# Output sums in place, full-height transposes at the end, constant products between the batches, and a new issue order, in a Branchformer block with its gradients

## The chip, the core and the metric

The kernel runs on one core of one Trainium2 chip. The metric is the time of one execution on the device, in microseconds (us); lower is better. The core has five engines with queues of their own: TensorE (PE in the profile, its weight loads PEld), VectorE (DVE), ScalarE (ACT), GpSimd (POOL) and SyncE (SP), which here issues nearly all DMAs. Each engine takes the instructions of its queue in order and waits on semaphores for the others.

## The reference, cut

The program computes a Branchformer block for 2 sequences of 4000 tokens with 144 channels, and the gradients of its input and of all seven weights: nine outputs.

```python
def _fwd_reference(x, w_qkv, w_att_out, w_mlp_in, dw_csgu, w_mlp_out, dw_merge, w_merge):
    xa = _layernorm(x, axis=-1)
    q, k, v = split(einsum('btd,de->bte', xa, w_qkv))
    scores = einsum('btd,bsd->bts', q, k) * D ** (-0.5)
    p = _softmax(scores, axis=-1)
    glob = einsum('btd,de->bte', einsum('bts,bsd->btd', p, v), w_att_out)
    h = _gelu(einsum('btd,de->bte', _layernorm(x), w_mlp_in))
    u, g = h[..., :D], _layernorm(h[..., D:])
    gc = sum over 5 taps of shifted g * dw_csgu[i]
    loc = einsum('btd,de->bte', u * gc, w_mlp_out)
    m = concat([glob, loc])
    m = m + sum over 5 taps of shifted m * dw_merge[i]
    return x + einsum('btc,cd->btd', m, w_merge)

def reference(..., grad_out):
    _out, _vjp = jax.vjp(_f, x, w_qkv, w_att_out, w_mlp_in, dw_csgu, w_mlp_out, dw_merge, w_merge)
    return (_out, *_vjp(grad_out))
```

## The kernel before

Tokens lie on 125 partitions, 32 blocks of 125 tokens to a batch (`NB`), in eight groups of four blocks (`GB`) where inputs are loaded or outputs stored. The two batches run one after the other, each in four stages.

*Preparation* (`pre_pieces`): x and grad_out are loaded; statistics on VectorE (`st`, `mv`), a power on GpSimd, the normalized rows on VectorE, GpSimd and, in the first batch, ScalarE (`ln`, L433 to L437); then transposes of the normalized rows (`xat`, L442 and L446) and of grad_out (`gm`, L400; `gs`, L407) on TensorE, with evictions by ScalarE and VectorE (L447, L408). Ahead of the first batch stands the head: weight products, and 111 constant products (`WARM`, L154) whose result nobody reads.

*Attention with its backward* (`phase_att`): for each of 32 query tiles the scores in four quads of 500 columns (L1026, with the 16 channels above 128 at L1032); the minimum of their negatives on VectorE (L1050, reduced at L1052); the exponentials on ScalarE (L1058, four to a tile); a DMA transpose of P (L1062); the products Y (L1082); P times dP (L1068 to L1073); a DMA transpose of S in two halves (`st0`, `st1`, L1253); the products Z (L1128); and the products X (L1173), which are summed into `acc` on VectorE (L1179). Pieces of the local branch (`local_units`) stand between them.

*Merge* (`class Merge`): the gradient matrix H is summed in PSUM (L1458) while `tr_pieces` transposes the merged rows (L1379, L1384, evicted by ScalarE). `out_g(g)` computes four blocks of the output: it loads x (L1547), forms 48 products (L1555 and L1557) into two PSUM tiles, adds x on VectorE (L1558) and stores (L1559). For the first batch it runs during the second batch's preparation and first query tiles. Loads use two buffers and sums two others, by turns. `dx_a` and `dx_b` form the gradient of x (L1583, L1584, L1586), `dm1` one weight gradient (L1533).

*Final* (`class Final`), after the second batch alone: weight gradients from H. `weights` and `transp` transpose weights of 144 rows in two parts, 128 rows and 16 (L1613, L1614, L1639, L1640, L1645, L1646); `dwm` (L1763 to L1785) runs twice, `qk` between.

All of this is emitted in one natural order, and then `Planner.plan` cuts the instructions into 7,033 groups, checks that `ORDER` names every group once, and chains the groups of each engine in the order that `ORDER` writes out. `ORDER` is a table of group numbers, stored as differences, one list for each of the five queues. A group on TensorE is a run of products into the same tile (up to 16), a quad (up to 8), or one constant product. So the table alone says which instruction each engine takes next; what an instruction waits for comes from the data. PSUM is in three pools: `ps_sg` (two buffers of two banks, for the quads), `ps_w` (three buffers, for nearly everything else) and `ps_yz` (one buffer, for Y and Z and for the constant products).

Two memory regions matter. `SX` holds S for three tiles, then the transposed P from column 12288, the transposed S from 16384 to 20480 and, from 20480, four slots of scaled q rows. In the merge the same columns hold merged rows, the output weights `VU` from 17384, the two x buffers from 19112 to 20264, and the two sum buffers from 20480 to 21632.

Of the kernel before, what the change touches and what calls it, by code (L numbers as in the profile page):

```python
# [8 lines left out]
BF = mybir.dt.bfloat16  # L9
F32 = mybir.dt.float32  # L10
# [5 lines left out]
D = 144  # L16
# [454 lines left out]
WARM = 111  # L471
# [251 lines left out]
for _s in """  # L723
PE 10 1 1 1 1 1 1 1 1 1 1 1 1 1 1 1 1 1 1 1 1 1 172 3 -174 1 1 1 174 2 11 -186 1 1 1 1 1 1 1 1 1 1 1 1 1 1 1 1 1 1 1 1 1 1 1 1 185 2 -186 1 1 1 1 1 1
# [663 lines left out]
class Merge:  # L1388
# [35 lines left out]
    def late_y(self):  # L1424
# [10 lines left out]
        o += 10 * D  # L1435
        self.VUs = [k.SX[0:80, o + D * h:o + D * (h + 1)] for h in range(2)]
        o += 2 * D
        self.xo = [k.SX[0:PB, o + GB * D * h:o + GB * D * (h + 1)].rearrange("p (a b) -> p a b", b=D) for h in range(2)]
        o = 20480
        self.o_ = [k.SX[0:PB, o + GB * D * h:o + GB * D * (h + 1)].rearrange("p (a b) -> p a b", b=D) for h in range(2)]  # L1440

# [347 lines left out]
def kernel(ctx, tc, x, w_qkv, w_att_out, w_mlp_in, dw_csgu, w_mlp_out, dw_merge, w_merge, grad_out,  # L1789
# [159 lines left out]
    for g in range(5, k.NG):  # L1949
        M.dx_a(g)  # L1950
    for g in range(k.NG):
        M.dx_b(g)
    M0 = M
    M.close()
    es_x0.close()

# [81 lines left out]
```

## Time and profile before

| | us |
|---|---|
| median of three runs | 1287.12 (1286.42 to 1287.43) |
| profiled execution | 1286.85 |
| its span, first to last instruction | 1285.1 |
| mean granted TensorE clock | 0.992 |
| idle before TensorE's instructions from 60 to 560 us, ended by another engine or a DMA | 3.6 |

The page gives busy time for each engine, the chain of work that ended last (followed back from the last instruction, at each step to what released it), and groups of instructions by line. A busy TensorE is not TensorE at its peak: its products are pipelined, and a product's own length (0.226 us for 144 columns) is longer than the step from one start to the next (0.062). Costs on TensorE are therefore read from starts. By stage, with times from the start of the span: head 0 to 40, first attention 40 to 575, first merge and second preparation 575 to 630, the first batch's output and the second attention's start 630 to 690, second attention to 1190, second merge and the final part to the end.

### The profile page before, as it was taken

How to read it: one execution, taken by the hardware profiler on the slowest of the kernel's cores; microseconds unless marked ns; L12 is line 12 of the kernel's file. 1: busy time of each engine (PE TensorE's matmuls, PEld its weight loads, DVE VectorE, ACT ScalarE, POOL GpSimd, SP SyncE). 2: the span in 40 equal slices, each digit the busy share in tenths (PEclk: the TensorE clock that was granted, in tenths of full speed). 3: DMA queues.
4: the chain of work that ended last, by engine and by line, in shares of the span. 5: the costliest groups of instructions: out<-in, count | busy, mean ns of one | idle time of the engine just before them, and what ended most of it. 6: DMA issues, size and time to landing. Idle time of an engine off the chain costs nothing.

```text
span 1285.1 us, 38822 instructions
## 1 busy us (share of the span) xinstructions
PE 1252.2 (97%) x15809; PEld 1037.1 (81%) x15809; DVE 1050.0 (82%) x2825; ACT 760.5 (59%) x1232; POOL 479.7 (37%) x971
## 2 busy tenths in 40 slices
PE   9999999999999999999888999999999999999996
PEld 7777888777888888899777788888878888888995
DVE  8698888978888988879668888888979798887755
ACT  5866656666666565536546665666666666555362
POOL 8544334333433342314524334433343343233020
PEclk9999999999999999999899999999999999999998
DMA  4698899998889998984349888999897988989612
GB/s 127 121 159 156 152 153 153 140 161 156 150 157 154 147 159 148 161 195 112 84 96 157 149 162 147 154 155 160 138 163 140 157 155 146 164 144 182 175 57 59
DMA packets 630206, 186.50 MB, mean 145 GB/s; under 512 B 612337, under 2 KB 624972, under 8 KB 630022
## 3 DMA queue, kind: packets, MB, share of 16 engines
q1 hardware_dynamic: 629271, 183.57, 78.8%
q8 instruction: 123, 2.02, 0.6%
q14 instruction: 56, 0.45, 0.1%
q0 software_dynamic: 208, 0.25, 0.1%
q10 hardware_dynamic: 548, 0.21, 0.1%
HBM read 20.82 MB, written 14.22 MB: 27 GB/s over the span
## 4 chain that ended last, share of the span: by engine, by line
PE 82%; DVE 10%; DMA 3%; issue 1%; ACT 1%; POOL 1%; SPq 0%; DVEq 0%; ACTq 0%; POOLq 0%
PE X L1173 20%; PE ps L1026 15%; PE yz L1128 9%; PE yz L1082 9%; PE ps L1032 6%; PE Hps L1458 4%; PE po L1555 3%; DMA SX<-SX 2%; DVE Pb L1050 2%; DVE acc L1179 1%; PE pj L989 1%; PE pc L607 1%; PE pw L667 1%; PE pd L555 1%; PE pd L622 1%
## 5 line engine op out<-in xcount | busy, mean ns | idle before, releaser
L1050 DVE TENSOR_SCALAR_CACHE_REDUCE Pb<-ps 125x1000 bf16<-125x1000 f32 x256 | 306.1, 1196 | 86.1 <-PE ps L1032 84.6
L1058 ACT ACTIVATE Pb<-Pb,nm 125x1000 bf16<-125x1000 bf16 x256 | 278.9, 1127 | 113.5 <-DVE nm L1052 113.2
L1173 PE MATMUL X<-SX 125*125 125x144 bf16 x2048 | 296.5, 229 | 1.6 <-ACT l_sq L523 0.8
L1173 PE MATMUL X<-SX,Pb 125*125 125x144 bf16 x2048 | 291.9, 226 | 0.2 <-POOL SX L1110 0.2
L1071 ACT CAST SX<-ps 125x1000 bf16<-125x1000 f32 x189 | 188.0, 994 | 158.3 <-PE ps L1032 156.3
L1173 PEld LDWEIGHTS <-SX 125*125 125x125 bf16 x2048 | 259.4, 137 | 25.2 <-issue 24.5
L1026 PE MATMUL ps<-xaT_m,qt 128*125 128x500 bf16 x1024 | 261.0, 375 | 2.1 <-DVE Pb L1050 1.7
L1173 PEld LDWEIGHTS <-Pb 125*125 125x125 bf16 x2048 | 260.4, 137 | 2.8 <-issue 2.4
L1179 DVE TENSOR_TENSOR acc<-X,acc 125x432 f32<-125x432 f32 (+1 forms) x372 | 199.1, 549 | 31.6 <-PE X L1173 29.6
L1128 PE MATMUL yz<-xa_aug,SX 125*125 125x144 bf16 x2048 | 152.1, 228 | 5.8 <-DMA SX<-SX 3.3
L1026 PEld LDWEIGHTS <-qt 128*125 128x125 bf16 x1024 | 122.3, 137 | 42.7 <-issue 4.0
L1128 PEld LDWEIGHTS <-SX 125*125 125x125 bf16 x2048 | 139.5, 138 | 13.7 <-issue 7.7
L1082 PE MATMUL yz<-xa_aug,SX 125*125 125x145 bf16 x2048 | 145.3, 227 | 1.0 <-DMA SX<-Pb 1.0
L1082 PEld LDWEIGHTS <-SX 125*125 125x125 bf16 x2048 | 136.5, 137 | 3.3 <-issue 2.0
L1073 DVE TENSOR_TENSOR SX<-SX,Pb 125x1024 bf16<-125x1024 bf16 x189 | 130.8, 695 | 7.7 <-ACT SX L1071 7.1
L1032 PEld LDWEIGHTS <-qt 16*125 16x125 bf16 x1024 | 36.5, 128 | 99.5 <-issue 99.5
L1032 PE MATMUL ps<-XR,qt 16*125 16x500 bf16 x1016 | 111.7, 420 | 0.0
L1068 DVE TENSOR_TENSOR SX<-ps,Pb 125x1000 bf16<-125x1000 f32 x67 | 80.0, 1194 | 9.0 <-ACT SX L1071 5.2
L650 POOL TENSOR_TENSOR A_dwc<-l_fl,A_dwc 128x512 f32<-128x512 f32 (+2 forms) x48 | 37.8, 787 | 85.6 <-ACT l_fl L649 85.6
L632 POOL TENSOR_SCALAR l_w<-gd,nc,c 125x144 f32<-125x144 bf16 x64 | 30.1, 475 | 87.8 <-DVE c L630 80.9
L1001 POOL COPY qz<-qz 125x48 bf16<-125x48 bf16 (+1 forms) x124 | 33.9, 289 | 66.2 <-ACT qz L991 65.4
L1555 PE MATMUL po<-SX 128*125 128x144 bf16 x640 | 54.1, 229 | 2.4 <-DVE SX L1558 2.4
(485 smaller groups left out, 2284.7 us busy)
## 6 DMA issues: line engine op xcount, KB each, us to landing
go_h<-in_grad_out_dram SPq DMA_DIRECT2D x4, 567.0 KB
Yg<-ug_d SPq DMA_DIRECT2D x4, 567.0 KB
Yn_d<-yn SPq DMA_DIRECT2D x64, 35.2 KB
Zn_d<-qz SPq DMA_DIRECT2D x64, 35.2 KB
ug_d<-ugr SPq DMA_DIRECT2D x32, 70.3 KB
SX<-in_x_dram SPq DMA_DIRECT2D x16, 140.6 KB
out_dram<-Pb SPq DMA_DIRECT2D x16, 140.6 KB
out_dram<-SX SPq DMA_DIRECT2D x16, 140.6 KB
```

What stands on the lines that cost most here:

```text
L1026: mm = nc.tensor.matmul(pp[r // 2][:, r % 2, 0:CH], QT[i][:, 3 * h, 0:PB], xaTm[:, c * CH:(c + 1) * CH], start=True, stop=False)
L1032: nc.tensor.matmul(pp[r // 2][:, r % 2, 0:CH], QT[i][rs, 1 + h, 0:PB], xr, start=False, stop=True)
L1050: nc.vector.tensor_scalar(pv(Pbuf, i % NPB, c2), src, -1.0, 3.0e38, op0=ALU.mult, op1=ALU.min, accum_out=NM[i][:, c2:c2 + 1])
L1058: nc.scalar.activation(v, v, ACT.Exp, bias=NM[i][:, 4:5], scale=-1.0)
L1068: nc.vector.tensor_tensor(pv(Sbuf, i % NDB, c2), src, pv(Pbuf, i % NPB, c2), op=ALU.mult)
L1071: nc.scalar.copy(pv(Sbuf, i % NDB, c2), src)
L1073: nc.vector.tensor_tensor(sc, sc, pchunk(i % NPB, c2), op=ALU.mult)
L1082: nc.tensor.matmul(Y, PT[0:PB, j, 0:PB], xaa[:, j, 0:D + 1], start=(j == 0), stop=(j == NB - 1))
L1128: nc.tensor.matmul(Z, ST[0:PB, j, 0:PB], xaa[:, j, 0:D], start=(j == 0), stop=(j == NB - 1))
L1173: nc.tensor.matmul(X[:, jj, :], l, r, start=(n_ == 0), stop=(n_ == len(ops) - 1))
L1179: nc.vector.tensor_tensor(av, X[:, 0:nj, :], av, op=ALU.add)
L1555: nc.tensor.matmul(po[:, q, :], self.yt(h, i + kk), VU[h][:, kk, :], start=(n_ == 0), stop=False)
```

## The change

Four edits, and a new table.

`out_g` adds into the x buffer itself, and takes one of four buffers by turns: the two at 19112 and the two at 20480 that held the sums. A load then overwrites a buffer whose store, four groups earlier, has to be done; in the kernel before it overwrote one that the add of two groups earlier had read.

```diff
-        self.xo = [k.SX[0:PB, o + GB * D * h:o + GB * D * (h + 1)].rearrange("p (a b) -> p a b", b=D) for h in range(2)]
-        o = 20480
-        self.o_ = [k.SX[0:PB, o + GB * D * h:o + GB * D * (h + 1)].rearrange("p (a b) -> p a b", b=D) for h in range(2)]
+        self.xo = [k.SX[0:PB, q + GB * D * h:q + GB * D * (h + 1)].rearrange("p (a b) -> p a b", b=D) for q in (o, 20480) for h in range(2)]
...
-        xo, o_ = self.xo[g % 2], self.o_[g % 2]
+        xo = self.xo[g % 4]
         nc.sync.dma_start(xo, tok_view(k.x, b)[:, b0:b0 + GB, :])
...
-            nc.vector.tensor_tensor(o_[:, 2 * p2:2 * p2 + 2, :], po[:], xo[:, 2 * p2:2 * p2 + 2, :], op=ALU.add)
-        nc.sync.dma_start(tok_view(k.out0, b)[:, b0:b0 + GB, :], o_)
+            nc.vector.tensor_tensor(xo[:, 2 * p2:2 * p2 + 2, :], po[:], xo[:, 2 * p2:2 * p2 + 2, :], op=ALU.add)
+        nc.sync.dma_start(tok_view(k.out0, b)[:, b0:b0 + GB, :], xo)
```

The transposes of `Final` take 128 rows in both parts; the 112 rows under the 16 are zero, and their columns of the result are not copied out.

```diff
-        pt = self.pt([128, 2, D], BF)
+        pt = self.pt([128, 2, 256], BF)
         for cc, (a, w) in enumerate(((0, 128), (128, DR))):
-            nc.tensor.transpose(pt[0:w, cc, 0:128], src[:, 0, c0 + a:c0 + a + w], ident[:])
-            nc.tensor.transpose(pt[0:w, cc, 128:D], src[0:DR, 1, c0 + a:c0 + a + w], ident[0:DR, 0:DR])
-        nc.scalar.copy(t[:, 0, :], pt[:, 0, :])
-        nc.scalar.copy(t[0:DR, 1, :], pt[0:DR, 1, :])
+            for q in range(2):
+                nc.tensor.transpose(pt[0:w, cc, 128 * q:128 * q + 128], src[:, q, c0 + a:c0 + a + w], ident[:])
+        nc.scalar.copy(t[:, 0, :], pt[:, 0, 0:D])
+        nc.scalar.copy(t[0:DR, 1, :], pt[0:DR, 1, 0:D])
...
-                pt = self.pt([128, D], BF)
-                nc.tensor.transpose(pt[:, 0:128], sWm[h][:, 0, kk, 0:128], ident[:])
-                nc.tensor.transpose(pt[:, 128:D], sWm[h][0:DR, 1, kk, 0:128], ident[0:DR, 0:DR])
-                (nc.scalar.copy if kk % 2 else nc.vector.tensor_copy)(t[:, kk, :], pt[:])
+                pt = self.pt([128, 256], BF)
+                for q in range(2):
+                    nc.tensor.transpose(pt[:, 128 * q:128 * q + 128], sWm[h][:, q, kk, 0:128], ident[:])
+                (nc.scalar.copy if kk % 2 else nc.vector.tensor_copy)(t[:, kk, :], pt[:, 0:D])
```

The same is done for the two transposes at L1645 and L1646. One constant product is taken from the head, and thirty are added between the batches, 288 columns each, from the identity and a head weight; nobody reads their result.

```diff
-WARM = 111
+WARM = 110
+WARM2 = 30
...
     for g in range(k.NG):
         M.dx_b(g)
+    k.PL.tag("warm")
+    warm = k.ps_yz.tile([PB, 2, D + 1], F32, tag="yz", name="warm")
+    for _ in range(WARM2):
+        nc.tensor.matmul(warm[:].rearrange("p a b -> p (a b)")[:, 0:2 * D], W.ident[:, 0:PB], W.VUT[:, 0, :], start=True, stop=True)
     M0 = M
```

`ORDER` is written anew for all five queues, 7,062 groups; the groups are those of before but for the constant products. On TensorE the order is as before from about 780 to 1140 us of the old execution, on VectorE, ScalarE and GpSimd nearly so; elsewhere most groups have changed places with neighbours. The thirty new products stand two behind `ztd` (573.24 in the old execution), three ahead of the transposes `gm0` (611.03), nine behind them, two ahead of `gm1` (614.46) and seven between it and `xat3` (615.90), two behind `gs2` (618.69), two behind `gm3` (620.87), and three between two products of the local branch near 634. In SP's queue the loads of `out_g` stand earlier and the stores of Yn, Zn and ug later.

More of the change, by code (lines that the diff above doesn't have):

```diff
@@ L723 @@
 for _s in """
-PE 10 1 1 1 1 1 1 1 1 1 1 1 1 1 1 1 1 1 1 1 1 1 172 3 -174 1 1 1 174 2 11 -186 1 1 1 1 1 1 1 1 1 1 1 1 1 1 1 1 1 1 1 1 1 1 1 1 185 2 -186 1 1 1 1 1 1
[32 rows of a table removed]
-DVE 9 112 -113 150 -14 29 7 -6 1 3 -1 11 -12 3 11 -8 -1 8 -6 1 1 1 9 -1 38 -1 -1 -37 -1 -1 22 -17 25 -22 16 2 2 52 -36 -38 1 39 -37 1 47 21 5 -41 1 2
[47 rows of a table removed]
-Activation 133 1 -4 2 -3 75 1 2 1 -77 5 -1 75 4 4 5 1 1 -13 34 89 -83 1 80 -72 -6 2 77 4 -2 5 -56 6 1 40 -32 -4 -2 43 -25 6 4 18 -1 -12 26 1 2 4 -2 3
[24 rows of a table removed]
-Pool 403 -234 1 -48 41 -39 21 2 15 253 -290 34 -33 -3 38 243 -258 -19 1 59 229 -251 51 4 -60 6 2 34 215 -246 88 4 -99 3 77 99 -117 76 -4 -15 63 82
[19 rows of a table removed]
-SP 0 1 2 -1 2 1 419 -274 275 1 -289 285 -416 421 -420 132 -1 13 98 -100 274 -275 -8 12 1 1 134 -38 -95 2 -1 -15 148 -146 347 -174 14 -15 -173 189 160
[16 rows of a table removed]
+PE 10 1 1 1 1 1 1 1 1 1 1 1 1 1 1 1 1 1 1 1 1 1 1 1 1 1 167 3 -169 1 1 1 1 1 1 1 1 1 1 162 2 11 -174 1 1 1 1 1 1 1 1 1 1 1 1 1 1 1 1 1 1 179 2 -180 1
[33 rows of a table added]
+DVE 9 111 23 -135 149 15 2 2 3 -2 1 -5 2 5 12 -5 -6 8 -6 11 -6 -6 2 1 8 -2 40 -2 -39 40 -18 -17 23 -2 4 -6 56 -36 34 -70 -1 -1 3 1 75 -28 -12 -3 41
[47 rows of a table added]
+Activation 132 -3 -1 5 1 1 -4 -1 76 -3 4 -3 5 13 -9 -2 6 6 109 5 -92 89 -83 85 -84 -28 111 -81 84 -82 4 73 -49 6 1 4 4 -6 18 6 4 18 1 -9 -5 26 1 2 4 1
[24 rows of a table added]
+Pool 168 -8 9 233 -243 -15 -21 291 -253 -3 245 -238 -3 -41 3 40 -42 24 -21 1 60 -59 18 74 -4 200 -248 -4 38 215 -250 96 -92 88 84 -99 54 4 -19 61 -20
[19 rows of a table added]
+SP 0 1 135 -134 1 135 286 -420 145 7 -151 1 420 -278 277 -418 130 284 -282 1 10 98 175 -1 -270 1 135 -137 4 132 -133 95 66 -173 172 -167 183 -189 188
[16 rows of a table added]
 """.strip().replace("\n ", " ").split("\n"):
@@ L1637, in weights @@
             for kk in range(5):
-                pt = self.pt([128, D], BF)
-                nc.tensor.transpose(pt[:, 0:128], sWm[h][:, 0, kk, 0:128], ident[:])
-                nc.tensor.transpose(pt[:, 128:D], sWm[h][0:DR, 1, kk, 0:128], ident[0:DR, 0:DR])
-                (nc.scalar.copy if kk % 2 else nc.vector.tensor_copy)(t[:, kk, :], pt[:])
+                pt = self.pt([128, 256], BF)
+                for q in range(2):
+                    nc.tensor.transpose(pt[:, 128 * q:128 * q + 128], sWm[h][:, q, kk, 0:128], ident[:])
+                (nc.scalar.copy if kk % 2 else nc.vector.tensor_copy)(t[:, kk, :], pt[:, 0:D])
             self.sT.append(t)
             ts = self.early.tile([80, D], BF, name="sTs%d" % h)
-            pt = self.pt([128, D], BF)
-            nc.tensor.transpose(pt[0:80, 0:128], sWr[h][:, 0, :], ident[:])
-            nc.tensor.transpose(pt[0:80, 128:D], sWr[h][0:DR, 1, :], ident[0:DR, 0:DR])
-            nc.scalar.copy(ts, pt[0:80, :])
+            pt = self.pt([128, 256], BF)
+            for q in range(2):
+                nc.tensor.transpose(pt[0:80, 128 * q:128 * q + 128], sWr[h][:, q, :], ident[:])
+            nc.scalar.copy(ts, pt[0:80, 0:D])
             self.sTs.append(ts)
```

277 rows, old and new, of the table ORDER are left out of this document.

## The prediction

> **What bounds the kernel now.** I read the page first: engine shares and the chain of work that ended last.
>
> ```profile
> PE 1252.2 (97%) x15809; PEld 1037.1 (81%) x15809; DVE 1050.0 (82%) x2825; ACT 760.5 (59%) x1232; POOL 479.7 (37%) x971
> PE 82%; DVE 10%; DMA 3%; issue 1%; ACT 1%; POOL 1%; SPq 0%; DVEq 0%; ACTq 0%; POOLq 0%
> ```
>
> TensorE is idle for only 1285.1 - 1252.2 = 33 us, and 82% of the chain is its products. An order of the same work can win only where TensorE waits, runs at half clock, or pays between products. So the second view was the busy time by stretch (PE, PEld, DVE, ACT, POOL, granted clock, DMA share, GB/s).
>
> ```profile
> 500.00:560.00 60.00, 59.68 (x769) 49.02 (x767) 46.03 (x111) 34.67 (x51) 19.52 (x41) 1.00 0.92 164
> 600.00:620.00 20.00, 16.95 (x242) 16.04 (x240) 17.70 (x50) 16.34 (x28) 12.27 (x14) 0.84 0.25 71
> 640.00:660.00 20.00, 17.97 (x208) 14.92 (x207) 11.88 (x32) 7.47 (x8) 3.42 (x7) 0.91 0.45 96
> 660.00:680.00 20.00, 17.01 (x204) 13.54 (x202) 14.47 (x37) 10.52 (x16) 7.46 (x13) 1.00 0.52 99
> 1240.00:1260.00 20.00, 20.00 (x300) 18.74 (x297) 7.53 (x23) 9.58 (x24) 1.97 (x3) 1.00 0.23 64
> 1272.00:1285.10 13.10, 2.87 (x14) 1.01 (x12) 5.51 (x32) 1.76 (x7) 1.27 (x1) 0.65 0.21 57
> ```
>
> Attention is full (500 to 560). The stretch between the batches is not: 3.05, 2.03 and 2.99 us idle in three rows, with the clock at 0.84 and 0.91 in two. The end is full up to 1272; from there a chain of TensorE and VectorE in turn (dwm, L1763 to L1780) takes 13.1 us. TensorE's waits between the batches, from the timeline (start, length, instruction, idle before it and who ended it):
>
> ```profile
> 611.03 0.60 PE L400 MATMUL pt<-ident,Pb 125*128 125x125 bf16 x8 [0.74 <-DVE R L447]
> 612.75 0.61 PE L442 MATMUL pt<-ident,xa_aug 125*128 125x125 bf16 x8 [1.12 <-DVE lnnm L428]
> 613.64 1.02 PE L407 MATMUL pt<-ident,go_r 125*80 125x125 bf16 x8
> ...
> 648.88 0.41 PE L1555 MATMUL po<-SX 128*125 128x144 bf16 x4
> 651.32 0.76 PE L1555 MATMUL po<-SX 128*125 128x144 bf16 x5 [2.03 <-DVE SX L1558]
> ```
>
> Eight transposes take 0.61 us at 612.75 and 1.02 at 613.64: the clock halves there. The chain of waits tells what the 2.03 us at 651.32 hang on, and SP's timeline why that load was late:
>
> ```profile
> 644.70 0.47 DVE SX L1558
> 645.18 0.28 SPq L1547
> 645.56 5.12 DMA SX<-in_x_dram
> 650.81 0.47 DVE SX L1558
> 651.32 0.76 PE po L1555 x5
> ```
>
> ```profile
> 641.59 0.27 SPq L1559 DMA_DIRECT2D out_dram<-SX  x1
> 645.18 0.67 SPq L1547 DMA_DIRECT2D SX<-in_x_dram  x2
> ```
>
> Two x loads leave together at 645.18. The second (og4, into the buffer that og2's add at 641.6 had freed) stood behind the first (og5), which waited for og3's add at 645.16. The last view is the end transposes:
>
> ```profile
> 1211.91 0.22 PE L1639 MATMUL fpt<-ident,goT 128*128 128x128 bf16 x1
> 1212.07 0.18 PE L1640 MATMUL fpt<-ident,goT 16*128 16x16 bf16 x1
> 1212.18 0.23 PE L1639 MATMUL fpt<-ident,goT 128*128 128x128 bf16 x1
> 1212.34 0.18 PE L1640 MATMUL fpt<-ident,goT 16*128 16x16 bf16 x1
> 1212.45 0.55 PE L1458 MATMUL Hps<-Yg,go_h 125*128 125x144 bf16 x6
> 1217.76 0.61 PE L1379 MATMUL pm<-ident,Yg 125*128 125x125 bf16 x8
> 1218.21 0.60 PE L1384 MATMUL pm<-ident,Yr 125*80 125x125 bf16 x8
> ```
>
> By starts, a pair of a 128-row and a 16-row transpose takes 0.27 us; eight full transposes take 0.45, 0.056 each.
>
> **The change, part by part.** *Out in place, four buffers.* A load now needs the store of four groups earlier, not the add of two earlier. In the new issue order og4's load stands right behind og1's store, 635.2 by the old times; og0's store had left at 631.41, and the add needs x at about 649.3. So the load has some 9 us after that store has landed, against 5.1 for the old load. The 2.03 us go, and so does the half clock that follows them: 24 products from 651.32 to 654.16 take 2.84 us, against 1.50 at full clock (the chain's pieces at 656.28, 656.66 and 657.03: six products each 0.375), and the quad behind them 1.24 against 1.04. That is 2.0 + 1.3 + 0.2 = 3.5 us. What is late next is the transpose of P: issued at 652.09, and if it takes as long as the chain's later one (9.37 us, issued at 677.92) it lands at 661.5, while Y's products, at 664.49 now, would be reached near 660. The cover is a moved reduction: L1052 ran at 645.78 though the last minimum ended at 643.79, behind an add, l_hg and the statistics; in the new order it follows that minimum at once, so the four exponentials and that issue come 2 us earlier. Without this cover 1.5 us come back. Range 0 to -3.5; I take -3.0, since the stall is removed by a condition that I can follow.
>
> Stores of og4 and og5 now read the buffers that lie where S's transpose is written (st1, L1253); og6 and og7 lie elsewhere. Now st1 is issued at 673.55, just after og7's add (673.47). After, it needs og7's products (670.25) and old stores, but stands behind st0 (to 672.05) and a store of 1.03 us. That is 0.5 us for Z's half, which waited 1.09 us; the new order also puts z1 behind a transpose that waited 1.66 us for a copy between partitions. Range -3 to +2 (waits of 668 to 688 sum to 5.3); I take -0.5.
>
> *Thirty constant products.* A 290-column one takes 0.124 us (median of starts at L154), so 30 take 3.7 us. 25 stand between 610 and 622 (3.1 us), where the waits sum to 0.74 + 1.12 + 0.39 + 0.38 + 0.42 + 0.18 + 0.60 = 3.8 us, twelve of them (1.5 us) in the first two, 1.86 us long. So nearly all lie in idle time; if that were gone they would cost up to 3.7 us. What they can win is the half clock from 613.7 to 620.5. The x transposes at 615.9 and 617.9 wait for the normalization on VectorE and GpSimd, and that stays: only the groups behind 617.2, some 3.3 us at half clock, can be quicker, by 1.6. VectorE's and ScalarE's evictions (0.69 and 0.99 us each) then take some of it back. Range +1.5 to -2.6; I take -1.2.
>
> When does the clock halve? After a stretch of 3.4 us with 1.86 idle (610.2 to 613.6: 45% busy, transposes alone) and after one with 2.03 idle (647.9 to 651.3: about 41% busy, real products). It was back at 620.5, by the lengths (1.04 at 619.53, 0.66 at 620.37), after 6.8 us of transposes with 1.19 idle. So transposes count for something. If they counted little, the nine constant products between those of 614 and 617 (1.1 us of 3.4, 33%) would be less than the 41% that did not hold the clock: a rival below. The Trainium skill ("TensorE: Matmul & The Clock Gate", "Part 4: PE-mode transpose") says that a transpose does not count as busy for the gate in the way a matmul does. By that rule this term would be 0 and the sum 1280.1; the recovery at 620.5 speaks against it.
>
> *End transposes.* 12 pairs (10 at L1639, 2 at L1645) go from 0.27 to 0.11 us: 12 x 0.16 = 1.9. Three calls of transp, two pairs each (0.52 us at 1217.24), go to 0.22: 0.9. Together 2.8 us on an engine that is 100% busy from 1200 to 1260. Behind it ScalarE evicts some 2 us late at 1227 but has 2.8 us free at 1235, so most arrives. Range 0 to -2.8; I take -2.5. The 13.1 us of tail are not touched, but the store that leaves last (out, 1281.00) now leaves before it: -0.3.
>
> *Table.* By slots and old times, TensorE's groups move by 0.3 to 0.8 us in the first batch and not at all from 780 to 1140; the head's one product less (0.12 us) lies in waits. TensorE's waits from 60 to 560 sum to 3.6 us, so the most to win there is that. In the head it waits for loads and normalization, whose order hardly moves: 0, ±2. First batch: -3.6 to +5 (below), I take -0.5: nothing moved there has a wait of its own that I can name.
>
> Sum: -3.0 - 0.5 - 1.2 - 2.5 - 0.3 - 0.5 = -8.0. The profiled execution took 1286.85 us, 1.75 of it outside the span, and is 0.27 below the median. 1286.85 - 8.0 = 1278.9; against the median, 1279.1. I say **1279**. Its own range is 1273 to 1284.
>
> **Rivals.** *The gap gives it back.* The stall leaves TensorE and reappears at the transposes of P and S, whose DMAs (5 to 9 us) set the pace from 664 to 688. For it: 5.3 us of waits there. Against: they start from work that moves up too. The gap then wins 0, the end 2.8: about **1284**.
>
> *The half clock stays near 614.* The constant products hold the clock up to 613.7, but the next 3.4 us have only 33% of real products and the wait for the normalization. Then the 1.2 us are not won: **1280**. For it: nothing but transposes stood in the halved stretch. Against: the clock came back during them.
>
> *Slower.* One mechanism, in SP's queue. In the first batch nearly all issues move (by 3 to 7 us on average), and a transpose of S or P behind a store that still waits comes late; Z's products then wait in order, with everything behind them. Price: the old trace has such waits of up to 1.1 us (Z for the transposed S). At 12 of 30 tiles it is +13 us; it decides from about 8 tiles on. With the -8: **1292**. For it: mean moves longer than a transpose. Against: most issues that I see moved back are stores of Yn, Zn and ug, which nothing waits for until the batch ends.
>
> *No change.* Order gains in a full engine cancel, and ScalarE's late evictions at the end take the rest: **1287**.
>
> **How the numbers follow.** Forecast 0.46, half clock stays 0.12, gap gives back 0.14, no change 0.11, slower 0.17. A measurement of this kernel tells 0.2% (2.6 us) from no change. So faster 0.46 + 0.12 + 0.14 = 0.72, same 0.11, slower 0.17. The range of 8 in 10 starts where the unknown terms take their far ends (0.5 + 2.5 + 1.4 + 0.3 + 3.1 = 7.8 below the forecast, and 1 of the head's 2) and reaches into the slower case: 1270 to 1290.
>
> **What would show it.** Right: no wait of L1555 for L1558 near 650; clock 1.00 from 600 to 660; L1639 and its partner 0.11 us a pair; the second batch's attention as full as before, only some 5 us earlier. Wrong: waits of L1128 and L1082 for DMAs in the first batch in many tiles; constant products after which TensorE is late; half clock again near 614; ScalarE as the releaser of TensorE between 1215 and 1240.

## The result, and the profile after

The changed kernel takes 1279.22 us (median of 6 runs, 1278.0 to 1281.01) against 1286.77 (6 runs, 1285.59 to 1289.31): a ratio of 0.9942, with a 95% interval of 0.9929 to 0.9954, or 7.5 us less. The profiled execution took 1280.24 us, its span is 1278.4. The forecast was 1279. But the sum came out right because errors in its terms cancelled: the head lost 3 us that the forecast did not have, and other terms won more than it gave them. That is what the rest is about.

The page's busy shares and its chain, of the changed kernel:

```profile
PE 1251.6 (98%) x15838; PEld 1040.0 (81%) x15838; DVE 1050.6 (82%) x2825; ACT 760.2 (59%) x1232; POOL 477.5 (37%) x971
PE 87%; DVE 6%; DMA 3%; POOL 1%; ACT 1%; issue 1%; SPq 0%; POOLq 0%; ACTq 0%; DVEq 0%
```

TensorE does the same 1252 us of work; the idle time around it fell from 33 to 27 us. Busy time by stretch, in the columns known from before (PE, PEld, DVE, ACT, POOL, granted clock, DMA share, GB/s):

```profile
600.00:620.00 20.00, 18.95 (x294) 18.33 (x292) 19.34 (x63) 17.55 (x30) 14.11 (x17) 1.00 0.13 37
620.00:640.00 20.00, 19.32 (x251) 17.64 (x249) 11.10 (x27) 12.58 (x29) 8.97 (x13) 0.91 0.32 100
640.00:660.00 20.00, 20.00 (x258) 16.55 (x257) 12.26 (x32) 8.03 (x9) 4.68 (x9) 1.00 0.52 105
660.00:680.00 20.00, 16.38 (x182) 12.47 (x181) 16.14 (x38) 10.29 (x16) 6.32 (x13) 0.98 0.57 117
680.00:700.00 20.00, 19.79 (x230) 16.69 (x229) 16.76 (x41) 13.12 (x23) 8.39 (x20) 0.93 0.92 169
```

The row 640 to 660 is full now (17.97 before). But half clock is still there: at 620 to 640, and in 680 to 700, where the old profile had none. TensorE's waits from 600 to 700 us (line, who ended it: us, times, longest):

```profile
PE ps L1028 <- DVE Pb L1052: 1.8, 2, 1.4
PE pt L589 <- DMA gd<-gd: 1.3, 1, 1.3
PE pt L442 <- DVE R L408: 1.0, 1, 1.0
PE pt L407 <- DVE R L447: 0.7, 1, 0.7
PE yz L1130 <- DMA SX<-SX: 0.4, 1, 0.4
```

The wait of out's products (L1555) for the add, 2.03 us at 651 before, is not among them. SP's timeline shows why: the x loads (L1547) leave one by one, the one at 637.02 right behind a store of out (L1559), and none in a pair behind a late add.

```profile
636.59 0.27 SPq L1559 DMA_DIRECT2D out_dram<-SX  x1
637.02 0.27 SPq L1547 DMA_DIRECT2D SX<-in_x_dram  x1
640.19 1.24 SPq L1010 DMA_TRANSPOSE qt<-qz  x1
641.48 0.47 SPq L1587 DMA_DIRECT2D out_dram<-Pb  x1
642.04 0.28 SPq L1547 DMA_DIRECT2D SX<-in_x_dram  x1
```

The end transposes run without the small partner. Four of them:

```profile
1211.62 0.39 PE L1640 MATMUL fpt<-ident,goT 128*128 128x128 bf16 x4
1211.85 0.79 PE L1458 MATMUL Hps<-Yg,go_h 125*128 125x144 bf16 x10
```

From start to start that is 0.23 us for two pairs, 0.115 a pair instead of 0.27.

**Where the time went.** The same groups of products run in both kernels, so one can take a group's start in the old trace minus its start in another: how far ahead that execution is there. Medians over TensorE's groups of the stretch behind the given old time, in us (ahead is positive); "end" is the old span minus the new. The rows behind the first are kernels of the experiments below.

```
old time           40   540   640   660   740  1180  1270   end
changed          -3.0  -2.9  -2.5   1.2   2.9   2.7   4.1   6.7
head_ident       -0.7  -1.4   0.4   4.2   6.9   6.4   8.3  11.0
head_old          0.1  -0.8   1.1   4.8   8.0   6.9   8.1  10.1
first_old         0.1   0.2   2.0   5.7   7.4   7.0   8.1  10.7
no_const         -3.3  -3.1  -2.6   1.1   0.3   0.6   2.2   4.2
head_no_const     0.0  -0.6   0.8   4.5   5.2   5.3   6.4   8.4
in place alone    0.0   0.0   1.2   3.9   3.7   3.9   3.9   3.9
rows alone        0.2  -0.9  -0.9   0.9  -0.3  -0.1   2.2   2.4
last_store       -2.9  -4.1  -2.7   1.0   1.6   1.6   2.6   2.7
```

The changed kernel starts by losing 3.0 us in the head. It wins 3.7 at 650, 1.7 from 660 to 740, 1.4 from 1180 to 1270, and 2.6 in the last 10 us. The forecast had nothing for the head and 0.3 for the last step.

**The head.** GpSimd's timeline in the changed kernel:

```profile
3.73 0.80 POOL L1857 DMA_DIRECT2D zdram<-SX  x1
4.53 0.78 POOL L1862 MEMSET A_dwc<- 128x784 f32 x1
6.98 0.54 POOL L963 DMA_DIRECT2D SX<-zdram  x1 [1.67 <-DMA zdram<-SX]
...
7.55 0.23 POOL L27 MEMSET ident<- 128x128 bf16 x1
...
8.46 0.31 POOL L28 TENSOR_SCALAR_AFFINE_SELECT ident<-ident 128x128 bf16<-128x128 bf16 x1
```

The new order puts a copy out of zdram (L963), which waits 1.67 us for the DMA that fills zdram, ahead of the identity matrix. In the old profile the identity was ready 2.9 us earlier, and TensorE used it at 6.34:

```profile
5.57 0.32 POOL L28 TENSOR_SCALAR_AFFINE_SELECT ident<-ident 128x128 bf16<-128x128 bf16 x1
```

```profile
6.34 0.22 PE L194 MATMUL hps<-ident,Pb 128*128 128x128 bf16 x1
```

TensorE needs the identity for its first weight transposes. In the changed kernel:

```profile
5.60 1.77 PE L154 MATMUL warm<-SX 128*125 128x290 bf16 x8
8.82 0.22 PE L194 MATMUL hps<-ident,Pb 128*128 128x128 bf16 x1 [1.45 <-POOL ident L28]
```

So they start 2.5 us later than before. And the idle time costs twice, since the clock halves behind it (granted clock is the third number from the end; the first two rows are of the old profile, the others of the changed kernel):

```profile
7.00:10.00 3.00, 3.00 (x27) 2.67 (x27) 2.81 (x18) 0.83 (x4) 2.53 (x6) 1.00 0.47 118
10.00:14.00 4.00, 4.00 (x43) 3.79 (x42) 2.98 (x14) 2.99 (x9) 3.92 (x7) 1.00 0.41 102
```

```profile
7.00:10.00 3.00, 1.55 (x13) 0.94 (x11) 1.79 (x11) 0.66 (x2) 2.79 (x10) 1.00 0.79 215
10.00:14.00 4.00, 4.00 (x25) 3.56 (x25) 3.26 (x18) 1.41 (x7) 3.99 (x8) 0.57 0.32 82
```

### The profile page after: what moved, and what is told of

Same layout as the page of the kernel before. It is cut to its first block, busy times and chain, and to the rows that moved or that the text cites. A ratio compares the mean times of both kernels' runs of the same rounds, so it can differ in the third digit from the quotient of the medians.

```text
span 1278.4 us, 38874 instructions
## 1 busy us (share of the span) xinstructions
PE 1251.6 (98%) x15838; PEld 1040.0 (81%) x15838; DVE 1050.6 (82%) x2825; ACT 760.2 (59%) x1232; POOL 477.5 (37%) x971
## 3 DMA queue, kind: packets, MB, share of 16 engines
q8 instruction: 124, 2.03, 0.6%
## 4 chain that ended last, share of the span: by engine, by line
PE 87%; DVE 6%; DMA 3%; POOL 1%; ACT 1%; issue 1%; SPq 0%; POOLq 0%; ACTq 0%; DVEq 0%
PE X L1175 21%; PE ps L1028 15%; PE yz L1130 10%; PE yz L1084 9%; PE ps L1034 7%; PE Hps L1458 4%; PE po L1555 3%; PE pc L608 1%; PE pj L991 1%; DVE Pb L1052 1%; DMA SX<-SX 1%; PE pd L556 1%; PE pd L623 1%; PE pw L668 1%; PE pw L683 1%
## 5 line engine op out<-in xcount | busy, mean ns | idle before, releaser
L1028 PE MATMUL ps<-xaT_m,qt 128*125 128x500 bf16 x1024 | 260.8, 375 | 3.8 <-DVE Pb L1052 3.4
L1181 DVE TENSOR_TENSOR acc<-X,acc 125x432 f32<-125x432 f32 x372 | 199.9, 548 | 32.0 <-PE X L1175 30.1
L1028 PEld LDWEIGHTS <-qt 128*125 128x125 bf16 x1024 | 122.1, 137 | 44.0 <-issue 5.5
L1130 PEld LDWEIGHTS <-SX 125*125 125x125 bf16 x2048 | 140.6, 138 | 11.2 <-issue 8.9
L526 POOL TENSOR_SCALAR l_a<-l_sq 125x576 bf16<-125x576 bf16 x32 | 23.1, 723 | 94.1 <-ACT l_sq L524 93.7
L1110 POOL TENSOR_SCALAR g<-qz,rl 125x144 f32<-125x144 bf16 x62 | 26.1, 421 | 84.0 <-DVE rl L1090 83.7
## 6 DMA issues: line engine op xcount, KB each, us to landing
SX<-in_x_dram SPq DMA_DIRECT2D x16, 140.6 KB
out_dram<-Pb SPq DMA_DIRECT2D x16, 140.6 KB
out_dram<-SX SPq DMA_DIRECT2D x16, 140.6 KB
```

The costliest lines, as they stand in the source:

```text
L1028: mm = nc.tensor.matmul(pp[r // 2][:, r % 2, 0:CH], QT[i][:, 3 * h, 0:PB], xaTm[:, c * CH:(c + 1) * CH], start=True, stop=False)
L1130: nc.tensor.matmul(Z, ST[0:PB, j, 0:PB], xaa[:, j, 0:D], start=(j == 0), stop=(j == NB - 1))
L1181: nc.vector.tensor_tensor(av, X[:, 0:nj, :], av, op=ALU.add)
```

## The experiments

Every ratio is to the kernel before, run on the same chip. 0.001 is 1.3 us. In the last column, only head_ident and last_store have intervals that do not touch the changed kernel's; the other differences from it are less sure.

```
kernel                 ratio    95% interval      against the changed kernel
changed                0.9942   0.9929 to 0.9954
head_ident             0.9910   0.9897 to 0.9923  -4.1 us
head_old               0.9922   0.9909 to 0.9934  -2.6
first_old              0.9918   0.9903 to 0.9933  -3.1
no_const               0.9960   0.9947 to 0.9972  +2.3
head_no_const          0.9928   0.9914 to 0.9942  -1.8
more_const             0.9931   0.9917 to 0.9946  -1.4
const_transposes       0.9925   0.9908 to 0.9942  -2.2
old_rows               0.9963   0.9947 to 0.9979  +2.7
rows_old_table         0.9979   0.9969 to 0.9989
in_place_old_table     0.9980   0.9971 to 0.9988
last_store             0.9969   0.9958 to 0.9981  +3.5
old_table_store        0.9953   0.9941 to 0.9965
```

**The identity moved ahead (head_ident).** On GpSimd alone:

```diff
 memset gd (L509)
 ...
+memset ident (L27)
 memset xa_aug (L1852)
 ...
 DMA zdram<-SX (L1857)
+select ident (L28)
 memset A_dwc (L1862)
 DMA SX<-zdram (L963)
 ...
-memset ident (L27)
 ...
-select ident (L28)
```

> The changed kernel, with two instructions moved in GpSimd's order: the identity matrix's memset and its select (L27, L28) stand ahead of the copies that wait for zdram, as they did before. In the changed kernel's profile TensorE idles 1.45 us from 7 to 10 us, its first weight transposes start at 8.82 instead of 6.50 us, the clock is halved from 10.3 to 13.7 us, and at 60 us its work stands 3.0 us behind the old kernel's. Theory (the table's new GpSimd order costs the head): the first transposes start near 6.5, no half clock before 20 us, and the whole is 3 to 4 us faster than the changed kernel: a ratio to before of 0.9911 to 0.9919 instead of 0.9942 (1275.5 to 1276.5 us). Rival (the head ends when the x loads and the normalization do, and the late transposes only fill another wait): the start moves, but the lead at 60 us does not, 0.9942 (1279.3). Rival (the profiled execution had a chance delay in the head): the lead at 60 us is as in the changed kernel's other executions and the ratio is within 0.001 of 0.9942.

0.9910, and the intervals of the two kernels do not touch. Its GpSimd timeline and stretches:

```profile
2.71 0.22 POOL L27 MEMSET ident<- 128x128 bf16 x1
...
4.77 0.32 POOL L28 TENSOR_SCALAR_AFFINE_SELECT ident<-ident 128x128 bf16<-128x128 bf16 x1
```

```profile
7.00:10.00 3.00, 3.00 (x27) 2.56 (x26) 1.78 (x11) 1.48 (x6) 2.53 (x8) 1.00 0.62 153
10.00:14.00 4.00, 3.59 (x34) 3.08 (x34) 2.84 (x16) 1.92 (x7) 3.76 (x8) 1.00 0.39 84
```

TensorE is full from 7 to 10 and the clock stays at 1.00. At 40 us it is 0.7 behind instead of 3.0. All four profiled kernels that kept the late identity (changed, no_const, old_rows, last_store) had half clock near 10 us, of 3.4 or 6.8 us; none of the others had. So it was no chance delay. The rest of the 4.1 us is less half clock later (none between 600 and 700 in this profile); that this part is chance is argued from the other profiles below.

**The old order up to 57 us (head_old).** On each queue the groups of the old order up to there (187 on TensorE, 118, 103, 114 and 50 on VectorE, ScalarE, GpSimd and SP), then the new order.

> The changed kernel with the old order on all five queues up to about 57 us of the old execution, the new order behind it. The run with the identity moved still had its work 0.7 us behind the old kernel's at 40 us; the run with the old head and first batch had 0.1 ahead. Theory (all that the head lost was its order): the lead at 40 us is 0.1, no half clock before 600 us, ratio 0.990 to 0.991. Rival (only the identity matters, the other 0.7 us are refilled by waits behind): as the run with the identity moved, 0.991 to 0.992.

The lead at 40 us is 0.1, and there is no half clock before 600, as expected. The ratio, 0.9922, is the rival's, and its interval only just reaches the theory's. The two together say that the head cost 2.6 to 4.1 us. By the leads at 40 us the identity makes 2.3 of the 3.1 us; what makes the other 0.8 is not shown, and the runs can't tell the two kernels apart.

**The old order in the head and the first batch (first_old).** As the last one, with 769, 1007, 567, 489 and 292 groups.

> The changed kernel with the old order in the head and in the first batch, on all five queues up to about 549 us of the old execution; the new order from there on. The run with the identity moved had its work 0.7 us behind the old kernel's at 20 us, 0.9 ahead at 250 and 1.4 behind at 540. Theory (the new order loses in the head by the identity, and loses another 1 to 2 us between 300 and 540): the lead at 540 us is 0 within 0.2, and the whole is 1.0 to 1.5 us faster than the run with the identity moved, 2.9 to 4 us faster than the changed kernel: ratio to before 0.9898 to 0.992. Rival (the first batch of the new order starts the gap's work earlier in other queues, and pays its loss back there): the lead at 540 is 0, but the lead at 700 is not above the 6.1 us of the run with the identity moved: 0.991. Rival (the prediction's step: the new first batch is worth 0.5 us): 0.5 us slower than the run with the identity moved, 0.9914.

The lead at 540 is 0.2, as expected, where head_old had lost 0.8 from 40 to 540. But the ratio, 0.9918, lies between those of head_ident and head_old, and the other profiles explain it: from 40 to 540 the lead changes by +0.2 to -1.2 in eight with the new order (mean -0.5; old_rows, with half clock at 78, left out), and by +0.1 to -1.1 in four with the old one (mean -0.3). But that sum hides two parts. By medians over the groups near 300 and near 600, all nine kernels with the new order fall back in between, by 0.9 to 2.6 us, and the four with the old one by nothing: the loss that the theory named is there. From 40 to 300 eight of the nine had won 0.4 to 1.4 us, and the old order gives that up too. So the new order of the first batch is on the whole neither a gain nor a loss that these runs can show.

**Without the constant products (no_const, head_no_const).** The first in the changed kernel, the second with the identity moved too; their thirty places in the order go.

```diff
-WARM2 = 30
+WARM2 = 0
```

> The changed kernel without its thirty constant products. The prediction's step: the products lie in idle time and hold the clock near 614. Then, without them, the half clock starts again near 614 and lasts 6.8 us instead of 3.4, and the whole is 1.2 us slower than the changed kernel (between 0 and 2.6): ratio 0.9951 (1280.4 us). Rival (the half clock has only moved from 614 to 621, and the products gain nothing): 0 to 0.5 us, 0.9942 to 0.9946. Rival (the products are in the way, as TensorE was late by then): 1 to 3 us faster, 0.992 to 0.9934.

> The changed kernel with the identity moved ahead on GpSimd and without the thirty constant products. The run without the products gave 0.996 (2.3 us slower than the changed kernel), but its profile did not lose them near 614: the clock was halved for 3.4 us at 621 in both, and at 679 for 6.8 us against 3.4. The run with the identity moved had no half clock in the gap and 0.991. Theory (the products hold the clock in 614 to 621, in most executions; which windows fall below half busy differs from execution to execution): a half clock of 3.4 to 6.8 us between 610 and 625, the mean granted clock 0.002 to 0.004 lower than with them, and 1.5 to 3 us slower than the run with the identity moved: 0.9922 to 0.9933. Rival (the 2.3 us were chance at 679): within 0.5 us of it, 0.991.

Both come out 2.3 us slower than their partners (the second against head_ident; against head_old it is 0.8), inside the theories' ranges, but the first not by its mechanism (its half clock stands at 621 for 3.4 us, as in the changed kernel, and not near 614 for 6.8), and the profiles do not let the products have all of it. The intervals of each pair overlap. What they do is seen in all profiles. Without them (before, in place alone, rows alone, old_table_store, no_const, head_no_const) there is half clock between 605 and 625 in 6 of 6, for 6.8 us once and 3.4 us else. With them it is 1 of 7 (the changed kernel itself). In time it is less. From 600 to 640 the leads grow by 1.45 us where the products held the clock, by 1.0 in the two kernels without, and by 0.0 in the changed kernel, where they didn't: there the products cost more than they won. The larger part of the difference of these two pairs arises at 675 to 690 us, where there are no constant products: half clock for 6.8 us in no_const, 3.4 in the changed kernel and head_no_const, none in head_ident. Over all profiles half clock stands at 670 to 690 in 4 of 7 with the products and in 4 of 6 without, so that part looks like chance. What the products are worth lies between 0.5 us (by the stretch in which they stand) and 2.3 (by the ratios), and is not settled.

**More of them (more_const).** head_old with eight more ahead of xat3 and five ahead of gs2.

```diff
-WARM2 = 30
+WARM2 = 43
```

> The changed kernel with the old order up to 57 us (as the run with the old head) and thirteen more constant products: eight more ahead of the transposes of xat3, which wait 1.05 us for VectorE, and five ahead of those of gs2, which wait 0.69. They take 13 x 0.124 = 1.6 us. Over all profiles so far, a stretch of 3.4 us of the clock's grid that was under 48% busy was always followed by half clock, one of 60% or more hardly ever; the two waits lie within 3.4 us, so with an unlucky position of the grid that stretch falls to 0.47 to 0.49 in the changed kernel. Theory (filled, it cannot): granted clock 1.00 from 605 to 625 us, no wait there ends later than before, and the whole is 0 to 1.7 us faster than the run with the old head (0.9922) or with the identity moved (0.991): 0.990 to 0.9915. Rival (the waits end earlier in most executions, so the products delay the transposes): xat3 starts later behind the last product, 0.5 to 1.5 us slower: 0.992 to 0.9934.

The first half of the theory holds. In its profile:

```profile
605.00:625.00 20.00, 19.85 (x285) 18.80 (x282) 17.67 (x46) 16.69 (x31) 12.05 (x15) 1.00 0.30 92
672.50:675.90 3.40, 1.68 (x12) 0.70 (x12) 3.14 (x7) 1.29 (x2) 1.85 (x5) 1.00 0.56 124
675.90:679.30 3.40, 2.26 (x17) 2.26 (x18) 3.04 (x6) 0.73 (x2) 0.00 (x0) 0.50 1.23 221
```

605 to 625 is nearly full (19.85 of 20.00) at clock 1.00, and from 600 to 640 the lead grows by 1.45 us as in head_old, so the extra products delay nothing. The time, 0.9931, is the rival's number, though not by its mechanism: here the half clock came at 676 and lasted 6.8 us, and the lead grew by 0.7 us from 660 to 740, where head_old's grew by 3.2. The expectation's "always" was not quite so by then: in the run with the new transposes alone, a stretch 48% busy was followed by full clock (shown under in_place_old_table).

**Transposes in their place (const_transposes).** On head_ident; two transposes in each place.

```diff
-WARM2 = 30
+WARM2 = 60
...
-    warm = k.ps_yz.tile([PB, 2, D + 1], F32, tag="yz", name="warm")
+    warm = k.ps_yz.tile([128, 2, 256], BF, tag="yz", name="warm")
...
-        nc.tensor.matmul(warm[:].rearrange("p a b -> p (a b)")[:, 0:2 * D], W.ident[:, 0:PB], W.VUT[:, 0, :], start=True, stop=True)
+        nc.tensor.transpose(warm[:, 0, 0:128], W.VUT[:, 0, 0:128], W.ident[:])
```

> The changed kernel with the identity moved ahead, and sixty transposes of a constant (128 x 128, 0.056 us each by the rows of other transposes, 3.4 us in all) in the places of the thirty constant products (3.7 us). It asks whether a transpose holds the clock as a product does. Theory (it does: in the run with the identity moved the stretch from 616.9 to 620.3 us was 55% busy, only 12% by real products, and the clock stayed at 1.00): the granted clock stays at 1.00 from 610 to 625 us and the ratio is that of the run with the identity moved, 0.991 (0.9905 to 0.9918). Rival (a transpose does not count): half clock of 3.4 to 6.8 us between 613 and 625, and the ratio of the run without the products, 0.9928 (0.992 to 0.994).

Not decided by this run: half clock came at 619, but the stretch of 3.4 us ahead of it was 47% busy, and stretches below 50% halve the clock with products too. The time (0.9925, from 0.9908 to 0.9942) fits both. Other profiles answer it better. Busy time of head_ident in one stretch, of all instructions and then of the transposes' tile pt alone:

```profile
616.88:620.29 3.41, 1.89 (x29) 1.75 (x29) 3.29 (x7) 2.49 (x4) 1.32 (x1) 1.00 0.47 195
620.29:623.70 3.41, 3.41 (x56) 3.27 (x54) 3.10 (x9) 2.93 (x5) 0.00 (x0) 1.00 0.55 140
```

```profile
616.88:620.29 3.41, 1.79 (x27) 2.17 (x4) 1.94 (x2) 1.00 0.47 195
```

The stretch is 55% busy, and all but 0.4 us of it with transposes alone (the two overlap a little). The clock stays at 1.00 in the next one. The run with the old transposes has such a stretch too (57% busy, 12% without transposes, clock 1.00 behind it). The changed kernel had the same work shifted by 0.5 us against the grid, and fell to 49%:

```profile
617.85:621.27 3.42, 1.69 (x26) 1.40 (x25) 3.39 (x8) 2.48 (x4) 1.75 (x2) 1.00 0.38 151
621.27:624.68 3.41, 3.41 (x33) 3.30 (x31) 2.01 (x5) 1.30 (x3) 0.00 (x0) 0.50 0.68 198
```

Clearer still are stretches with transposes and nothing else, which the kernels without constant products have. In in_place_old_table one is 79% busy (all instructions, then tile pt alone, then the next stretch), and the clock stays at 1.00:

```profile
616.83:620.25 3.42, 2.72 (x43) 2.42 (x43) 3.33 (x9) 2.32 (x3) 0.27 (x1) 1.00 0.55 208
616.83:620.25 3.42, 2.72 (x43) 1.37 (x2) 1.99 (x2) 1.00 0.55 208
620.25:623.66 3.41, 2.41 (x38) 2.36 (x37) 2.23 (x8) 3.41 (x8) 1.48 (x1) 1.00 0.32 115
```

So transposes alone can hold the clock.

**The old transposes (old_rows), and the new ones alone (rows_old_table).** The first undoes the edit in the changed kernel, the second makes it in the old one.

```diff
-            for q in range(2):
-                nc.tensor.transpose(pt[0:w, cc, 128 * q:128 * q + 128], src[:, q, c0 + a:c0 + a + w], ident[:])
+            nc.tensor.transpose(pt[0:w, cc, 0:128], src[:, 0, c0 + a:c0 + a + w], ident[:])
+            nc.tensor.transpose(pt[0:w, cc, 128:D], src[0:DR, 1, c0 + a:c0 + a + w], ident[0:DR, 0:DR])
...
```

> The changed kernel with the end transposes as they were, 128 rows and then 16 (same order of groups). The prediction's step: 15 of the pairs' 18 cost 0.27 instead of 0.11 us, 2.5 us slower than the changed kernel (0 to 2.8): ratio 0.9961 (1281.8 us). Rival: the end's gain of 4.0 us in the profiles (the lead grows from 2.7 to 6.7 us behind 1180 us) comes from the new order there and not from the rows: under 1 us, 0.9942 to 0.995. Rival: it comes from the rows alone, the tail included: 3.5 to 4 us, 0.997.

> The kernel before with the end transposes over 128 rows and nothing else. Prediction's step: 2.5 us faster (0 to 2.8): ratio 0.998. The run with the old transposes in the changed kernel gave 0.9963 against 0.9942, 2.7 us. Rival (in the old order ScalarE's evictions are late at 1227 us and take it back): 0 to 1 us faster, 0.9992 to 1.0000; ScalarE or VectorE would be the releaser of TensorE's waits between 1215 and 1262.

2.7 us slower in the one, 2.7 us faster in the other (0.9979), against 2.5 forecast. In the second's profile the lead steps from -0.1 at 1180 to 2.2 at 1270. So the step holds in the old order. In the new one it is less sure: the intervals of old_rows and of the changed kernel overlap, and by the leads the transposes give 1.7 us there (from 1180 to 1270 the changed kernel wins 1.4, old_rows loses 0.3).

**Out in place alone (in_place_old_table).** The old kernel and order, with:

```diff
-        xo, o_ = self.xo[g % 2], self.o_[g % 2]
+        xo = self.xo[g % 4]
...
```

> The kernel before with out summed in place in four buffers, and nothing else: its old order, its old transposes, no constant products. The prediction's step is that the wait of 2.03 us at 651 (and 1.3 + 0.2 us of half clock behind it) hangs on the load of og4, which is late. Here the two loads stand behind og2's store as before but wait for stores that left at 631 and 635 instead of og3's add at 645.2, so they can leave at 641.9, 3.3 us earlier. Theory (the buffers alone remove the wait): no wait of L1555 for the add near 650, clock 1.00 from 640 to 660, and 3.0 us faster than before (1 to 3.5): ratio 0.9977. Rival (the gap gives it back at the transposes of P and S at 664 to 688 us, since only the new order starts them earlier): the wait is gone at 651 but the lead at 740 us is under 1 us: 0.9992 to 1.0000.

0.9980, 2.6 us. The loads leave at 640.73 instead of 645.18, but a wait of 0.93 us stays at 649, with another cause. The chain of waits:

```profile
646.35 0.72 POOL rsr L544
647.38 1.19 DVE Pb L1050 x2
648.57 0.38 DVE SX L1556
649.00 0.47 PE po L1553 x5
```

The add (L1556 here, L1558 before) now waits on VectorE behind a minimum (L1050, 1.19 us), which itself stands behind statistics that wait for GpSimd (rsr, L544). In the old profile the same minimum ends at 649.80, and the add then waits another 1.01 us for the load. In the changed kernel VectorE's order is another, and nothing is left. So the buffers remove 1.1 of the 2.03 us, the new order the rest. The half clock behind the wait is not certain: with the transposes alone, the wait is still there (1.78 us at 651.93), the stretch of the clock's grid that holds it (649.40 to 652.81) is 48% busy, and yet the row shows clock 1.00:

```profile
640.00:660.00 20.00, 18.22 (x228) 14.68 (x226) 13.66 (x33) 7.94 (x9) 4.19 (x8) 1.00 0.60 102
```

That the runs give 2.6 us, more than the 1.1 us of the wait, fits half clock that goes with it in most executions, but this is not shown.

**One store last again (last_store).** In SP's order of the changed kernel:

```diff
-store out, group 6 (L1559)
 store out, group 7 (L1559)
 ...
 store db (L1785)
+store out, group 6 (L1559)
```

> The changed kernel with one DMA moved: the store of out's group 6 is the last of SP's queue again, as before, where the changed kernel has it 6 us ahead of the end. In the old profile the span ends 4.4 us after the second last store is issued, in the changed one 2.5 us after the last. The prediction gave this 0.3 us. Theory (the last store's landing sets the end, and out's takes longer): 1.5 to 1.9 us slower than the changed kernel, ratio 0.9954 to 0.9957 (1280.8 to 1281.1 us). Rival (the prediction's 0.3 us, since the rest of the difference is the clock at the end): 0.9944.

3.5 us slower (0.9958 to 0.9981), of which the end itself is 2.5: the lead goes from 2.6 at 1270 to 2.7 at the end, where the changed kernel's goes from 4.1 to 6.7. SP's last DMAs, first in the changed kernel and then in this one:

```profile
1275.49 0.33 SPq L1776 DMA_DIRECT2D out_dram<-Pb  x1
1275.91 0.27 SPq L1785 DMA_DIRECT2D out_dram<-Pb  x1
```

```profile
1277.62 0.33 SPq L1637 DMA_DIRECT2D out_dram<-Pb  x1
1278.04 0.27 SPq L1646 DMA_DIRECT2D out_dram<-Pb  x1
1278.37 0.29 SPq L1420 DMA_DIRECT2D out_dram<-SX  x1
```

Behind the last issue the span goes on for 2.5 us in the first (to 1278.4), and for 4.1 in the second (to 1282.4): the store of 140.6 KB takes 1.6 us longer to end than the small one, and leaves 0.3 later. So it is in the other profiles too: 4.1 us in the four whose last store is that of out, 2.5 in the ten that have a small one last. Most of the other 0.6 is half clock: the last four products of L1763 take 1.21 us here and 1.38 in the old profile, against 0.62 in the changed one.

**The three cheap edits in the old order (old_table_store).** In place, rows, and the store of group 6 behind that of group 7.

> The kernel before, in its old order, with three edits: out in place in four buffers, end transposes over 128 rows, and the store of out's group 6 behind that of group 7 instead of last in SP's queue (all its sums are done by 1271.8 us of the old execution, the store leaves at 1281.0). Measured alone: in place 2.6 us, rows 2.7 us; the store 2.5 us by the profiles (4.4 against about 2 us from the second last store's issue to the span's end). Theory (the three add up, and the rest of the new table is a wash: its gap and products win what its head loses): 7.3 to 8 us faster than before, ratio 0.9938 to 0.9943, as the changed kernel. Rival (they share the same waits, so only the new order lets them add): 4 to 6 us, 0.9953 to 0.9969.

0.9953, 6.0 us: between the two theories, on the rival's edge, with an interval (0.9941 to 0.9965) that reaches both. Its lead steps by 2.6 at 650, 2.3 from 1180 to 1270 and 2.6 at the end, as in the kernels that have one of them, and loses 0.9 at 675 to 690, where the clock was halved for 3.4 us. So the steps do add up. The changed kernel, with its whole new table and the products, is 1.4 us faster than this one, which the intervals can't tell from nothing.

## The prediction, point by point

- *"In the head it waits for loads and normalization, whose order hardly moves: 0, ±2."* The step that failed. The head lost 3.0 us, in the profile and by the runs. Most of it, 2.3 us by the leads, came from GpSimd's order and not from TensorE's: one small instruction came 2.9 us later (8.46 instead of 5.57), behind a copy that waits for a DMA. What the new order of the other queues adds (0.8) stays open. The prediction followed SP's queue and TensorE's and costed GpSimd's at nothing.
- *Out in place, -3.0.* The lead grows by 3.7 at 650: the wait of 2.03 and the half clock behind it. The mechanism, the late load, is confirmed, but the load was not all of it: the buffers alone leave 0.93 us, behind a minimum on VectorE that the prediction did not name, and only the new order removes that. The cover it named is there: the reduction of the minima follows the last minimum at once (646.77 and 646.88), and the transpose of P is issued 5.3 us behind that minimum (652.18) instead of 8.3. The 1.5 us of half clock are no fixed saving: in rows_old_table the clock stayed full behind nearly the same wait.
- *Z and the transposes of S, -0.5.* From 660 to 740 the lead grows by 1.7, in spite of 3.4 us of new half clock; without that, in head_old, by 3.2. The waits for the transposed S and P fell from 2.9 to 0.4 us, while those of the scores for the minima (L1028) rose from 0.4 to 1.8. Right in sign, too small.
- *Constant products, -1.2.* Costless where the clock held (13 more of them in more_const delayed nothing), but not in the changed kernel, where it halved all the same. There half clock stands at 621, as in no_const without them, so the sign named (clock 1.00 from 600 to 660) failed, and the rival of a half clock that stays has its share; in six other profiles with the products the clock was 1.00 from 600 to 660. 0.5 to 2.3 us over many executions, open. The rule of the Trainium skill ("TensorE: Matmul & The Clock Gate", "Part 4: PE-mode transpose"), by which a transpose doesn't count as busy in the way a matmul does, is not borne out: a stretch 79% busy with transposes alone held the clock at 1.00 (in_place_old_table), and so did one 55% busy, nearly all of it transposes (head_ident).
- *End transposes, -2.5.* 2.7 by the runs, as a part taken out and as a part put in; by the leads 2.3 in the old order and 1.7 in the new.
- *Last store, -0.3.* 1.9 to 2.6: the mis-sized term. What sets the end is when the last transfer has landed, and the large store needs 1.6 us more for that than the small one. The forecast counted only the issues, 0.33 us apart.
- *First batch, -0.5.* 0.1 in this execution; -1.2 to +0.2 over eight. A term within the noise, made of a gain ahead of 300 us and a loss behind it.
- *The rivals.* SP's order didn't delay the first batch (one wait of 0.5 us for a DMA from 60 to 560). The gap gave some back, as half clock at 679 and as waits for the minima, but kept more than it lost. From 1200 to 1240 no wait of TensorE was ended by ScalarE.
- *The second batch's attention some 5 us earlier.* It runs 2.7 to 2.9 us ahead: without the head's loss it would be nearer 6.

Made from the leads, the sum is +3.0 (head), -0.5 (40 to 640), -3.7, -1.7, +0.2 (740 to 1180), -1.4 and -2.6: -6.7 us for this execution. The median of all executions gives -7.5. A total that agrees says little about the terms: the head lost 3.0 us that the forecast had at nothing, and everything behind it won 9.7 where the forecast had 8.0. That these nearly cancelled is luck.

The fastest kernel measured is the changed one with the identity moved back ahead, at 0.9910 (0.9897 to 0.9923) of the old time, faster than both kernels; head_old, with the whole old head, gave 0.9922 (0.9909 to 0.9934).

## What to carry to other kernels

When an order is written anew, go through every queue for the one small instruction that a whole engine waits for, and ask what it now stands behind: an identity matrix behind a copy that waits for a DMA cost 3 us here, about as much as the best single edit won (2.7 us). At the end of a kernel, let the largest store go before the small ones, and count until it has landed, not until it is issued. A saving that goes through a halved clock isn't a fixed number of one profile: look at several executions before you book it.

## What was not expected of the hardware

The granted clock changes only on a grid of 3.41 us, and the grid lies elsewhere in each execution against the kernel's work. The Trainium skill ("TensorE: Matmul & The Clock Gate", "What's actually happening") calls the window free-running and gives it 3413 ns; the traces agree on both. What they add is the measure: over the 14 profiles, of the stretches of the grid at full clock in which TensorE was under 49.5% busy (transposes counted) 31 of 32 were followed by half clock, of those from 49.5% to 59.5% 5 of 23, of those from there to 75% 1 of 50. So a wait of 1.7 us within one stretch is nearly always enough; the one exception is the 1.78 us of rows_old_table. Two short waits within 3.4 us, like those at 617 to 621 and at 671 to 680, halve the clock in some executions and not in others. Single runs of one kernel differ with their granted clock: const_transposes took 1274.4 us in the run with 0.998 and 1280.8 in that with 0.993, a spread larger than most edits of this change.
